# Where the result transposes and the FFN2 tiles live in PSUM: a block-sparse attention and FFN kernel on one core

## The chip, the cores and the metric

One Trainium2 chip, one NeuronCore. The metric is the device time of one execution in microseconds. The kernel before took 329.12 us (median of three runs, 328.71 to 329.84). TensorE, VectorE, ScalarE, GpSimd and the queue engine are written PE, DVE, ACT, POOL and SP, as in the profile.

## The reference

```python
scores = scale * np.matmul(q, k.transpose(0, 1, 3, 2))   # B 4, H 8, S 768, D 64
mask = (|blk_i - blk_j| <= 1) | first/last block row or column | 3 sampled blocks per block row
attn = softmax(np.where(mask, scores, -1e9));  attn_out = attn @ v
x = attn_out.transpose(0, 2, 1, 3).reshape(3072, 512)
h = x @ w_in;  g = 0.5 * h * (1.0 + erf(h * inv_sqrt2));  out = g @ w_out   # d_ff 2048
```

Blocks are 32 positions; a block row sees 8 blocks of keys (first, last, three around it, three sampled), only the first and last block rows see all 24.

## The kernel before

Every engine executes its own queue in the order in which the program is written (`manual_schedule`); the tile pools only add the semaphore waits. So the order in which the Python functions call each other is the order on each engine, and an engine that waits holds up all that is behind it in its queue.

**Units.** The work is cut into nine units of query rows: units 0, 1 and 2 are the three parts of batch 0 (128, 256 and 384 rows), then two units of 384 rows per batch. Units 0, 3, 5 and 7 are "dense": they also compute the first and last block row. A quad is 128 rows, four blocks.

**Stages.** The main loop runs over n = 0 to 8. Stage n computes FFN1 of unit n (`ffn1_step`, eight steps of eight products and one gelu on ACT), then `attention` of unit n+1, into which the FFN2 products of unit n are strewn as filler: `ffn2_pieces` yields once per product (16 products of 128x512 make one quad's output tile `op`), and `fill(m)` takes m of them. The lists in QUOTAS and in the last lines of the loop say how many pieces go behind each iteration (quota, the first entry for iteration -1) and how many into the tail behind the last one. After attention the pieces left are run, then FFN1 of unit n+1 begins; its first product needs all of the transposed attention result xT.

**One attention.** A round is two block rows of one quad, or for dense units one block row and half the heads; I write S, E, T for a round's scores (PE, L287), exponentials (ACT, L324, four per round) and transposes of the probabilities (DVE, L341/345), V for the product of probabilities and values of a group (PE, L387 or L363), F for filler pieces (PE, L447). Rounds count from 0. A group is the two rounds of one quad (g0, g1, g2), or the four dense rounds (d). Iteration `it` of `attention` issues, each on its engine: S of round it+1; V of a group that is two rounds old; T of round it-1; the maxima (DVE, L312/315) of round it+1; the division (DVE, L400 to 404, tile xh) of the group just weighed; E of round it; hooks; filler; and `outputs` of the group that was weighed the iteration before. `outputs` transposes xh on PE (L414) into the PSUM tile `tx`, and ACT copies it to xT (L419, L424). Behind the loop stand the load of the gelu table on ACT, the last T, the V of the last group, and the last `outputs`.

**PSUM.** Eight banks: psA (two tiles of two banks: scores and FFN1 results), psV (one tile of two banks, `av`: the values), psT (one bank: `tx`), psO (one bank: `op`). A pool with one buffer makes the next writer wait for the last reader of the tile before.

**The store.** When the last piece of a quad's tile is issued, `store` at once issues the copy `os<-op` on ACT (L439) and the DMA on SP (L441).

**Gathers.** Sampled blocks are copied by number into the tile gb (`gather`, L251), three copies per block row, mostly on DVE; the block numbers come from registers (`block_numbers`). For unit 2, six block rows are gathered during FFN1 of unit 1 and five in hooks of its attention (QUOTAS n = 1). GpSimd gathers four block rows for unit 1 at the start. GpSimd also issues all loads, each of which can wait for an older one.

**In front of stage 0.** Unit 0's attention runs alone with no filler; its hook at iteration 5 puts a large copy on ACT (`kvs[0][:, :, 0:KC]` from k0, L545).

**The end.** `last_output` computes FFN2 of unit 8 without anything beside it: two full quads and one in two halves, in four banks.

Of the kernel before, what the change touches and what calls it, by code (L numbers as in the profile page):

```python
# [9 lines left out]
F32 = mybir.dt.float32  # L10
# [9 lines left out]
def kernel(  # L20
# [22 lines left out]
    V2 = 2 * VW  # L43
    KC = NPR * BL
# [19 lines left out]
    psT = ctx.enter_context(tc.tile_pool(name="psT", bufs=1, space=PSUM))  # L64
    psO = ctx.enter_context(tc.tile_pool(name="psO", bufs=1, space=PSUM))
# [50 lines left out]
    def load_w_out(part, n=2):  # L116
        w = KOUT // n
        nc.gpsimd.dma_start(
            out=w_out_sb[:, w * part:w * part + w, :],
            in_=moe_w_out[P * w * part:P * w * (part + 1)].rearrange("(ko p) f -> p ko f", p=P))  # L120
# [92 lines left out]
    def spaces():  # L213

        views = [psT.tile([P, PI, PP], BF16, name="pt", tag="T")]
        two = psV.tile([P, 2, 1024], BF16, name="pq", tag="V")
        views += [two[:, i, 0:S].rearrange("p (i c) -> p i c", i=PI) for i in range(2)]
        return views + [psO.tile([P, PI, PP], BF16, name="pt", tag="op")]
# [176 lines left out]
    def divided(grp):  # L395
# [11 lines left out]
        st[grp, "xh"] = xh, n, m  # L407

    def outputs(unit, grp):
        xh, n, m = st.pop((grp, "xh"))  # L410
        T = psT.tile([P, 4, P], BF16, name="tx", tag="T")
        for h in range(2):
            for G in range(m // 2):
                nc.tensor.transpose(T[:, 2 * G + h, 0:32 * n],  # L414
                                    xh[0:32 * n, h, P * G:P * G + P],
                                    identity[0:32 * n, 0:32 * n])
        if grp[0][0] == "s":
            xT, t0 = column[unit.b, grp[0][1][0]]
            nc.scalar.copy(xT[:, :, t0:t0 + 32 * n], T[:, :, 0:32 * n])  # L419
        else:  # L420
            Tv = T[:, 0:2, :].rearrange("p h (g x q) -> p g h x q", g=2, x=2)
# [5 lines left out]
    def ffn1_step(n, m):  # L427
# [6 lines left out]
        nc.scalar.activation(g[:, m:m + 2, 0:T], hp[:, :, 0:T], AF.Gelu)  # L434
# [7 lines left out]

    def ffn2_pieces(n):
        for t, quad in enumerate(units[n].quads):
            op = psO.tile([P, D_MODEL], F32, name="op")
            for m in range(KOUT):
                nc.tensor.matmul(op, lhsT=g[:, m, t * P:(t + 1) * P], rhs=w_out_sb[:, m, :],  # L447
                                 start=(m == 0), stop=(m == KOUT - 1))
                if m != KOUT - 1:
                    yield  # L450
            store(n, quad, slice(0, D_MODEL), op)
            yield

    def last_output(n):
# [5 lines left out]
        banks = [psO.tile([P, D_MODEL], F32, name="op"), two[:, 0, :], two[:, 1, :],  # L460
                 psT.tile([P, D_MODEL], F32, name="op", tag="T")]
# [7 lines left out]
    def attention(unit, filler, quota, tail, held=0, hooks=None):  # L469
# [14 lines left out]
        for it in range(-1, n):  # L484
# [11 lines left out]
            if it >= 0:  # L496
                exponentials(rounds[it])
            for f in hooks.get(it, ()):
                f()
# [4 lines left out]
        while due and due[0][0] < n - 1:  # L504
            divided(weigh())
            if len(given) > 1:
                outputs(unit, given.pop(0))
        turned(rounds[n - 1])
        fill(tail[0])
        divided(weigh())  # L510
        while len(given) > 1:
            outputs(unit, given.pop(0))
        fill(tail[1])
        outputs(unit, given.pop(0))
        for _ in filler:
            pass

# [15 lines left out]
    for part in range(2):  # L533
        load_w_out(part)
# [12 lines left out]
    QUOTAS = {0: ([0, 2, 4, 4, 1], (1, 2)), 1: ([6, 5, 5, 4, 3, 2, 2], (1, 2))}  # L547
    for n, unit in enumerate(units):
# [3 lines left out]
        hooks = {}  # L552
        if nxt is not None and not fresh:
# [4 lines left out]
            elif n == 1:  # L558
                known |= block_numbers(J1[:6], DVE)
                gather(nxt, J1[:6], known)  # L560
                for it, (i0, i1) in enumerate(((6, 9), (9, 11))):
                    hooks[it] = [lambda u=nxt, js=J1[i0:i1]: gather(u, js, block_numbers(js, DVE))]
# [4 lines left out]
        for s in range(KOUT // 2):  # L567
            ffn1_step(n, 2 * s)
            if s == 0:
                if n == 0:  # L570
                    hold_loads(0)
                    for h in range(H):
                        load_v(1, h)
                if n > 0 and not fresh and b + 1 < B:
# [29 lines left out]
        elif n in QUOTAS:  # L604
            attention(nxt, filler, *QUOTAS[n], hooks=hooks)
        elif fresh:
            attention(nxt, filler, [5, 5, 6, 4, 4, 4, 4, 2, 2, 2, 0], (2, 5))
        else:
            attention(nxt, filler, [8, 8, 5, 5, 6, 2, 2], (3, 6))
# [30 lines left out]
```

## Time and profile before

| | us |
|---|---|
| profiled execution, device time | 329.59 |
| its span in the profile | 327.8 |
| median of the timed runs | 329.12 |
| PE busy | 269.1 (82%) |
| DVE busy | 220.1 (67%) |
| ACT busy | 218.9 (67%) |
| POOL busy | 52.6 (16%) |
| granted TensorE clock, mean | 0.984 |

The span is what the trace covers; 1.8 us of the device time lie around it. The stretches of the span, cut near the first product of each FFN1 and the end of the last one (us, PE busy in brackets): unit 0 with the start 33.6 (17.1); FFN1 of unit 0 5.6; attention of unit 1 15.7 (9.5); FFN1 of unit 1 7.6; attention of unit 2 20.6 (14.3); then three times FFN1 14.8 to 15.0, dense attention 28.5, 28.5 and 26.7 (22.4, 23.0, 21.4), FFN1 10.5 to 11.1, sparse attention 19.2, 19.0 and 19.7 (16.8, 16.9, 17.1); and the last output, 14.8. In the FFN1 stretches PE is busy all the time; in the attentions it is not.

In the views below a line of the timeline has start, length, engine, source line, operation, operands, count, and in brackets how long the engine had been idle and what released it. A line of the waits has who waited for whom, the total in us, how often, and the longest.

### The profile page before, as it was taken

What the parts mean: (1) busy time and instruction counts of PE and PEld (TensorE: products, weight loads), DVE (VectorE), ACT (ScalarE), POOL (GpSimd) and SP (SyncE); (2) the same over time, 40 slices, a digit from 0 to 9 for tenths busy, and PEclk for the clock granted to TensorE, in tenths of its full rate; (3) what the DMA queues carried; (4) which work ended last, traced back from release to release, by engine and by line L of the source; (5) the groups of instructions that cost most, each with busy time, mean ns of one, the idle gap of its engine ahead of it and who ended that gap; (6) DMA issues with size and microseconds to landing.
All of it is one profiled execution on the core that took longest, in us unless ns stands there. A gap on an engine that the chain in (4) does not pass through costs nothing.

```text
span 327.8 us, 12763 instructions
## 1 busy us (share of the span) xinstructions
PE 269.1 (82%) x5582; PEld 155.8 (48%) x5624; DVE 220.1 (67%) x553; ACT 218.9 (67%) x378; POOL 52.6 (16%) x100
## 2 busy tenths in 40 slices
PE   1756776967999769988999779988999679979994
PEld 0515624634553445545653445545653445445643
DVE  6497764786597778586597778485698778584000
ACT  9668673767478674686477775686577775777521
POOL 8565900300520002300510002100000000000000
PEclk9999979999999988999999998999999999999999
DMA  7999994930790000930890001911000000000001
GB/s 113 139 123 207 208 113 41 153 76 4 69 64 32 36 4 34 149 80 36 71 62 32 34 6 37 187 39 37 34 3 32 36 4 34 1 36 36 32 34 64
DMA packets 39337, 20.74 MB, mean 63 GB/s; under 512 B 25841, under 2 KB 36338, under 8 KB 39282
## 3 DMA queue, kind: packets, MB, share of 16 engines
q0 software_dynamic: 35680, 13.63, 62.8%
q1 hardware_dynamic: 3602, 6.29, 5.0%
q8 instruction: 44, 0.72, 1.0%
q14 instruction: 11, 0.09, 0.1%
HBM read 27.26 MB, written 6.29 MB: 102 GB/s over the span
## 4 chain that ended last, share of the span: by engine, by line
PE 58%; DVE 15%; ACT 13%; issue 6%; DMA 5%; POOL 1%; DVEq 1%; ACTq 0%; POOLq 0%
PE hp L432 25%; PE op L447 13%; ACT pp L324 8%; PE av L387 6%; DVE pT L341 4%; DVE nm L312 4%; PE sc L287 3%; DMA w_in_sb<-in_moe_w_in_dram 3%; DVE xh L404 3%; DMA kv<-in_v_dram 2%; DVE kv L204 2%; PE av L465 2%; PE pt L193 2%; PE op L465 2%; ACT L351 2%
## 5 line engine op out<-in xcount | busy, mean ns | idle before, releaser
L324 ACT ACTIVATE pp<-sc,nm 128x256 bf16<-128x256 f32 (+1 forms) x192 | 91.8, 592 | 13.6 <-DVE nm L312 11.3
L432 PE MATMUL hp<-xT,w_in_sb 128*128 128x384 bf16 (+2 forms) x576 | 89.3, 312 | 1.2 <-ACT xT L419 0.9
L447 PE MATMUL op<-w_out_sb,g 128*128 128x512 bf16 x295 | 80.3, 390 | 9.4 <-issue 4.8
L434 ACT ACTIVATE g<-hp 128x768 bf16<-128x768 f32 (+2 forms) x72 | 53.2, 739 | 39.6 <-PE hp L432 39.4
L432 PEld LDWEIGHTS <-w_in_sb 128*128 128x128 bf16 x576 | 53.4, 100 | 32.1 <-issue 3.2
L312 DVE TENSOR_REDUCE nm<-sc 128x4 f32<-128x1024 f32 (+1 forms) x48 | 53.3, 1113 | 11.3 <-PE sc L287 10.7
L251 DVE COPY gb<-kv 128x388 bf16 (+1 forms) x252 | 46.0, 262 | 10.2 <-issue 8.6
L447 PEld LDWEIGHTS <-g 128*128 128x128 bf16 x336 | 28.5, 100 | 37.5 <-issue 15.5
L387 PE MATMUL av<-kv,pT 64*32 64x130 bf16 x1760 | 35.0, 229 | 12.8 <-DVE xh L404 5.4
L387 PEld LDWEIGHTS <-pT 64*32 64x32 bf16 x2816 | 29.0, 93 | 23.7 <-DVE xh L404 9.6
L341 DVE STREAM_TRANSPOSE pT<-pp 128x512 f32<-128x512 f32 (+1 forms) x48 | 31.6, 658 | 11.4 <-ACT pp L324 11.0
L287 PE MATMUL sc<-gb,qT 64*32 64x256 bf16 x704 | 19.7, 283 | 15.2 <-ACT pp L324 14.9
L287 PEld LDWEIGHTS <-qT 64*32 64x32 bf16 x832 | 10.8, 90 | 42.9 <-issue 29.1
L419 ACT COPY xT<-tx 128x512 bf16<-128x512 bf16 (+1 forms) x24 | 13.2, 552 | 23.6 <-PE tx L414 23.6
L439 ACT COPY os<-op 128x512 f32<-128x512 f32 (+1 forms) x23 | 13.3, 576 | 19.7 <-PE op L447 15.4
L124 POOL COPY mark<-g 1x1 bf16<-1x1 bf16 x6 | 3.6, 594 | 137.1 <-ACT g L434 137.0
L107 POOL DMA_DIRECT2D kv<-in_v_dram x32 | 22.8, 720 | 5.4 <-DMA w_out_sb<-in_moe_w_out_dram 3.5
L387 PE MATMUL av<-gb,pT 64*32 64x130 bf16 x1056 | 21.3, 230 | 1.4 <-issue 1.3
L351 ACT ACT_TABLE_LOAD x17 | 21.8, 1283 | 0.3
L404 DVE TENSOR_TENSOR xh<-av,rec 128x512 bf16<-128x512 f32 (+2 forms) x28 | 18.3, 652 | 1.0
L400 DVE TENSOR_SCALAR den<-av 128x8 f32<-128x8 f32 (+2 forms) x28 | 4.4, 155 | 21.2 <-PE av L387 20.7
L315 DVE TENSOR_REDUCE nm<-sc 128x1 f32<-128x768 f32 x16 | 15.3, 955 | 4.2 <-PE sc L287 4.0
(63 smaller groups left out, 212.8 us busy)
## 6 DMA issues: line engine op xcount, KB each, us to landing
out_dram<-os SPq DMA_DIRECT2D x23, 256.0 KB, 2.0
kn<-in_k_dram POOLq DMA_DIRECT2D x8, 384.0 KB, 5.5
qn<-in_q_dram POOLq DMA_DIRECT2D x8, 384.0 KB, 8.0
kv<-in_v_dram POOLq DMA_DIRECT2D x32, 96.0 KB, 7.7
w_in_sb<-in_moe_w_in_dram POOLq DMA_DIRECT2D x4, 512.0 KB, 12.7
w_out_sb<-in_moe_w_out_dram POOLq DMA_DIRECT2D x2, 1024.0 KB, 20.4
out_dram<-os SPq DMA_DIRECT2D x2, 128.0 KB, 1.7
raw<-in_sampled_blocks_dram SPq DMA_DIRECT2D x1, 0.6 KB
```

Of the source, the lines that this page charges most:

```text
L107: nc.gpsimd.dma_start(out=kvs[b % 2][32 * hh:32 * hh + 32, 0:NB, c0:c0 + D], in_=v[b, h].rearrange("(n p) d -> p n d", p=BL))
L251: (engine or nc.vector).tensor_copy(sampled(unit.place[j], r)[:, None, c0:c1], src[:, bass.ds(at[j][r], 1), :])
L287: nc.tensor.matmul(o, lhsT=qT[rows, pr, BL * j:BL * j + BL], rhs=rhs(rows, pr), start=True, stop=True)
L312: nc.vector.tensor_reduce(out=nm[:, 0:2 * n].rearrange("p (g j) -> p g j", g=2), in_=A4[:, :, 0:n, :], op=ALU.max, axis=AX.X, negate=True)
L324: nc.scalar.activation(dst.rearrange("p (c k e) -> p c e k", e=2, k=BL), src.rearrange("p (c e k) -> p c e k", e=2, k=BL), AF.Exp, bias=bias)
L341: nc.vector.transpose(pt[:, 0:w].bitcast(F32), pp[:, 0:w].bitcast(F32))
L351: nc.scalar.activation(junk, zero[0:1, 0:1], func)
L387: nc.tensor.matmul(av[32 * s:32 * s + 32, h, V2 * G:V2 * G + V2], lhsT=pv[rows, c // 2, :, c % 2], rhs=src[rows], start=(c == 0), stop=(c ...
L404: nc.vector.tensor_tensor(xh[rows, :, 0:m * D].rearrange("p h (x d) -> p h x d", d=D), a[:, :, :, 0:D], rec[rows, :, 0:m, None].to_broadca ...
L432: nc.tensor.matmul(hp[:, i, 0:T], lhsT=w_in_sb[:, ki, (m + i) * P:(m + i + 1) * P], rhs=xTs[n % 2][:, ki, 0:T], start=(ki == 0), stop=(ki ...
L434: nc.scalar.activation(g[:, m:m + 2, 0:T], hp[:, :, 0:T], AF.Gelu)
L447: nc.tensor.matmul(op, lhsT=g[:, m, t * P:(t + 1) * P], rhs=w_out_sb[:, m, :], start=(m == 0), stop=(m == KOUT - 1))
```

## The change

1. psT is gone. The transposed results go into free columns of the value tile itself: `av` has two banks of 512 columns, the values use 260 of each, and the transposes use 128 columns from column 264 on.
2. psO has two buffers. A finished tile is put on a list and copied out later: behind the exponentials of the next iteration, or at the latest when another tile has been finished.
3. The gelu of the last FFN1 step is two instructions, one for each half.
4. For unit 2, four block rows are gathered on GpSimd behind the value loads of stage 0, and one more on DVE before the attention; the hooks of its attention are gone.
5. w_out is loaded in four parts instead of two.
6. In the tail all given groups are put out before the next one is weighed, and all quotas and tails are new.

```diff
+    TX = 4 * VW + 4
-    psT = ctx.enter_context(tc.tile_pool(name="psT", bufs=1, space=PSUM))
-    psO = ctx.enter_context(tc.tile_pool(name="psO", bufs=1, space=PSUM))
+    psO = ctx.enter_context(tc.tile_pool(name="psO", bufs=2, space=PSUM))
...
-    def load_w_out(part, n=2):
+    def load_w_out(part, n=4):
...
-        views = [psT.tile([P, PI, PP], BF16, name="pt", tag="T")]
+        views = [psO.tile([P, PI, PP], BF16, name="pt", tag="op")]
...
-        T = psT.tile([P, 4, P], BF16, name="tx", tag="T")
+        T = av[:, :, TX:TX + P].bitcast(BF16).rearrange("p h (g t) -> p g h t", g=2)
         for h in range(2):
             for G in range(m // 2):
-                nc.tensor.transpose(T[:, 2 * G + h, 0:32 * n],
+                nc.tensor.transpose(T[:, G, h, 0:32 * n],
...
-        nc.scalar.activation(g[:, m:m + 2, 0:T], hp[:, :, 0:T], AF.Gelu)
+        for i in ((0, 2),) if m < KOUT - 2 else ((0, 1), (1, 2)):
+            nc.scalar.activation(g[:, m + i[0]:m + i[1], 0:T], hp[:, i[0]:i[1], 0:T], AF.Gelu)
...
+    finished = []
+
     def ffn2_pieces(n):
         for t, quad in enumerate(units[n].quads):
+            store_finished(1)
             op = psO.tile([P, D_MODEL], F32, name="op")
...
-                if m != KOUT - 1:
-                    yield
-            store(n, quad, slice(0, D_MODEL), op)
-            yield
+                if m == KOUT - 1:
+                    finished.append((n, quad, slice(0, D_MODEL), op))
+                yield
+
+    def store_finished(left=0):
+        while len(finished) > left:
+            store(*finished.pop(0))
...
-        banks = [psO.tile([P, D_MODEL], F32, name="op"), two[:, 0, :], two[:, 1, :],
-                 psT.tile([P, D_MODEL], F32, name="op", tag="T")]
+        banks = [psO.tile([P, D_MODEL], F32, name="op") for _ in range(2)] + [two[:, 0, :], two[:, 1, :]]
...
             if it >= 0:
                 exponentials(rounds[it])
+            store_finished()
...
         table(AF.Gelu)
-        while due and due[0][0] < n - 1:
-            divided(weigh())
-            if len(given) > 1:
-                outputs(unit, given.pop(0))
         turned(rounds[n - 1])
         fill(tail[0])
-        divided(weigh())
-        while len(given) > 1:
-            outputs(unit, given.pop(0))
+        while due:
+            while given:
+                outputs(unit, given.pop(0))
+            divided(weigh())
         fill(tail[1])
         outputs(unit, given.pop(0))
         for _ in filler:
             pass
+        store_finished()
...
-    for part in range(2):
+    for part in range(4):
         load_w_out(part)
...
-    QUOTAS = {0: ([0, 2, 4, 4, 1], (1, 2)), 1: ([6, 5, 5, 4, 3, 2, 2], (1, 2))}
+    QUOTAS = {0: ([4, 4, 2, 2, 1], (1, 1)), 1: ([6, 5, 5, 4, 3, 1, 1], (3, 2))}
...
-                for it, (i0, i1) in enumerate(((6, 9), (9, 11))):
-                    hooks[it] = [lambda u=nxt, js=J1[i0:i1]: gather(u, js, block_numbers(js, DVE))]
+                gather(nxt, J1[6:7], block_numbers(J1[6:7], DVE))
...
+                    gather(units[2], J1[7:], block_numbers(J1[7:], POOL), engine=nc.gpsimd)
...
-            attention(nxt, filler, [5, 5, 6, 4, 4, 4, 4, 2, 2, 2, 0], (2, 5))
+            attention(nxt, filler, [4, 4, 4, 4, 4, 4, 3, 3, 2, 2, 1], (6, 4))
-            attention(nxt, filler, [8, 8, 5, 5, 6, 2, 2], (3, 6))
+            attention(nxt, filler, [8, 8, 5, 5, 5, 2, 2], (6, 4))
```

## The prediction

> **What bounds the kernel now.** I read the busy line and the windows by stage first, then the waits, then the timeline of one stage of each kind.
>
> ```profile
> PE 269.1 (82%) x5582; PEld 155.8 (48%) x5624; DVE 220.1 (67%) x553; ACT 218.9 (67%) x378; POOL 52.6 (16%) x100
> ```
>
> PE is the busiest engine, and in the FFN1 stretches it never rests. What can be won or lost lies in the attentions, where PE idles 5 to 6 us in a dense one, 2 to 3 in a sparse one of batches 1 to 3, and 6 in unit 2's.
>
> ```profile
> ACT xT L419 <- PE tx L414: 23.6, 17, 3.1
> PE sc L287 <- ACT pp L324: 16.7, 20, 2.6
> ACT os L439 <- PE op L447: 15.4, 16, 2.2
> PEld L387 <- DVE xh L404: 9.6, 9, 1.8
> PE op L447 <- ACT os L439: 4.0, 12, 0.4
> ```
>
> The third and fifth lines are what the second bank aims at: ACT stands at a copy of op until the tile is done (15.4 us), PE waits 4.0 us for those copies. The fourth is the present price of one value bank: V of the next group waits until xh has been read out of it.
>
> The start of stage 0, then a sparse attention, then a dense one, from the timeline:
>
> ```profile
> 26.93 2.86 ACT L545 COPY kv<-qT 128x3200 bf16<-128x3200 bf16 x1
> 28.91 0.62 PE L387 MATMUL av<-kv,pT 64*32 64x130 bf16 x28 [0.32 <-DVE pT L341]
> 29.81 1.28 ACT L351 ACT_TABLE_LOAD   x1
> 31.10 0.20 ACT L351 ACTIVATE junk<-zero 1x1 bf16<-1x1 bf16 x1
> 31.46 0.43 ACT L424 COPY xT<-tx 128x128 bf16<-128x128 bf16 x2 [0.16 <-PE tx L414]
> 33.61 5.17 PE L432 MATMUL hp<-xT,w_in_sb 128*128 128x128 bf16 x64 [0.68 <-ACT xT L419]
> ```
>
> ```profile
> 148.96 0.59 PE L447 MATMUL op<-w_out_sb,g 128*128 128x512 bf16 x2 [0.44 <-ACT os L439]
> 149.39 0.38 PE L414 MATMUL tx<-identity,xh 128*128 128x128 bf16 x4
> 149.71 0.42 PE L387 MATMUL av<-kv,pT 64*32 64x130 bf16 x32
> 150.36 0.60 ACT L419 COPY xT<-tx 128x512 bf16<-128x512 bf16 x1
> ```
>
> ```profile
> 258.40 0.58 ACT L439 COPY os<-op 128x512 f32<-128x512 f32 x1 [2.16 <-PE op L447]
> 258.88 1.72 ACT L324 ACTIVATE pp<-sc,nm 128x256 bf16<-128x256 f32 x4
> 263.53 0.34 PE L414 MATMUL tx<-identity,xh 96*128 96x96 bf16 x4
> 264.09 0.49 ACT L419 COPY xT<-tx 128x384 bf16<-128x384 bf16 x1
> ```
>
> In the first and second of these, V of the next group (L387) starts before ACT has copied the transposes of the group before it. With T in the same tile as av it can't: the order of instructions after the change puts an ACT wait on the first V product of every group behind another. That is the step I follow.
>
> **Unit 0: +2.9 us.** ACT's queue stays: the copy L545 (26.93 to 29.79), the gelu table and its junk activation (to 31.30), then the two xT copies of group d (0.43). V of g0 now waits for them: 31.3 + 0.43 + 0.06 (ACT to PE, as 33.56 to 33.61) = 31.8 against 28.91. V takes 2.1 us as before, and xh, transposes, copy and FFN1 follow in a chain without slack. So 2.9 later, nothing hides it: there is no filler, and the next stages start from here.
>
> **Sparse attentions of units 4, 6, 8: +1.1 us each.** I follow unit 4. What goes: the waits for os at both tile changes (0.33 and 0.44), and 0.38 at S3, since E1 no longer stands behind os. What comes first: ACT now runs E0, E1, os, E2. E0 starts at 139.5 (0.1 late, below), lasts 1.67; E1 to 142.85; os 0.59; E2 1.66, to 145.1, so S4 starts at 145.15 against 145.37. F5, S5 and F2 follow: transposes of g0 at 148.75 against 149.39, 0.24 of which is one piece less in the quota. Then the copy: it starts 0.44 after the first transpose (154.35 to 154.79), lasts 0.58, and 0.06 later V of g1 starts, at 149.8 against 149.71. Left: +0.1 and one piece owed (0.24). In the tail the transposes of g1 now stand between V of g1 and V of g2, and PE waits the same 0.7 (1.08 less 0.38 of transposing) once more: V of g1 to 151.05; eight pieces to 153.1; V of g2 at 154.2, and with 1.05 for 96 products to 155.25; four pieces, 1.0, are less than the 1.3 that den, rec and xh take (154.35 to 155.63), so the last transposes start at 156.6; three pieces cover the copy, FFN1 at 157.65. Before it was 156.78 with 0.45 of "issue" idle inside V of g2; +0.9 without and +1.3 with such a stall: 1.1.
>
> **Dense attentions of units 3, 5, 7: +0.7 us each.** Unit 7 (granted clock 1.00). E2 starts at 250.05, not 250.75, and E6 at 257.1, not 258.88 (the os copies are no longer ahead of them); S8 moves from 260.65 to 259.45, V of g0 to 260.05 (waiting 0.2 for its copies), S9 from 262.55 to 261.75. Up to here 0.8 is won, though with fewer pieces done. Now V of g1: the copy of g0's transposes stands on ACT behind E8 and the second os (order after the change): E8 from 261.8 to 263.5, os to 264.05, copy to 264.55, V of g1 at 264.6, while PE was done at 263.2. V of g1 ends at 265.85, before 265.68, and 34 pieces are done, not 38. Tail as above: seven pieces to 267.65, transposes, copy (table loaded by 267.85) to 268.7, V of g2 to 270.0, xh to 271.3, transposes, copy, FFN1 at 272.4 against 271.74.
>
> **Unit 1: +0.3.** S3 comes 0.6 earlier (two pieces ahead of it, not four), E3 ends at 47.6, but V of g1 must wait for table (1.48) and copy (0.48): 49.75 against 49.47.
>
> **Unit 2: -1.2.** The nine hook copies (66.50, 1.76 with 1.04 of register loads before them) held T0 and so the maxima of round 2 from about 66.65 to 68.81; the six others cost about 0.9 again. Twelve copies go to POOL, three (0.6, and some 0.4 of register load) ahead of the attention, where the table load (62.73 to 64.01) hides them. With E2 at 67.95, E3 at 70.2, E4 at 71.9, V of g1 starts at 74.25 against 75.88. Then the tail's copy wait and xh chain: FFN1 at 81.3 against 83.15, or 82.3 without the 0.86 "issue" idle there; between -1.9 and -0.5, I take -1.2.
>
> **Small edits.** The gelu: 128x512 takes 597 ns, 128x256 384, so 171 are fixed; two halves cost 171 more, less an overlap of up to 155 (exponentials of 546 follow each other every 0.39). Only the first half has a wait on PE in the order after the change, so it waits for the whole step: 0 to +0.1, hidden mostly behind fillers, and counted above; -0.3 a stage if I misread the wait. w_out in quarters: before, it landed at 38.2 and 44.2; two more issues (0.88 each) delay POOL's gathers to about 28.4, before the 29.85 at which they wait for ACT anyway: nothing. POOL copies: 283 ns at 128 columns and 415 at 260 give about 0.54 at 388; twelve are 6.5 us at about 46 to 53, needed at 70: nothing. End: the fourth bank now waits for a copy of half a tile (0.37) where the third waited for a whole one (0.59): -0.2.
>
> **Sum.** 2.9 + 3 x 1.1 + 3 x 0.7 + 0.3 - 1.2 - 0.2 = 7.2. Against the profiled execution's 329.59 that is 336.8; the median lies 0.47 below that execution, so I predict 336 us.
>
> **Rivals.**
> *Half of it (330 to 332).* Unit 0's wait stands, but the tails cost nothing, because the "issue" stalls (1.19 at 118.5, 0.45 at 153.2) fall into the new waits. For: the tails hold such stalls. Then 2.9 + 0.3 - 1.2 - 0.2, about +2: 331.5. Chance 0.15.
> *Faster, 326.* ACT's relief is the larger part. If ACT reaches the copies so early that V never waits, which decides from 1.4 us ahead of my schedule in a dense stage and 0.7 in a sparse one, the leads worked out above remain: 0.8 at S9, 0.64 at the first transposes, and 2.3 in unit 2: 2.9 + 0.3 - 0.2 - 2.4 - 1.9 - 2.3 = -3.6. For: 15.4 us of ACT idle time. Against: the copies stand behind exponentials and table in ACT's queue. Chance 0.17; 0.06 more that the two balance.
> *POOL and DVE get in each other's way.* A DVE copy begun beside a POOL copy at 33.87 took 0.94 us where a like one right after took 0.78, so up to 0.2 a copy; the twelve would have to slip by 4 us to meet the fixed gathers of unit 2. Worth up to 12 x 0.2 = 2.4, 339. Chance 0.02.
> The Trainium skill (SBUF — State Buffer, Who interferes with whom) has a harder rule: a VectorE copy in a two-port mode and a GpSimd instruction lock each other out for a whole instruction. By it twelve collisions would cost 12 x 0.54 = 6.5 us, and the sum would be 343; the trace shows no full lockout, since five DVE copies of 128x384 beside POOL's copies (32.2 to 33.8) average 340 ns and two without them 336.
>
> **Chances and range.** The forecast, 332.5 to 340: 0.60. A measurement of this kernel tells about 0.3% from no change. Slower 0.60 + 0.15 + 0.02 = 0.77, same 0.06, faster 0.17. The range from 328.5 to 340 leaves out most of the faster case and little above.
>
> **What would show it.** The first FFN1 product near 36.5 instead of 33.61, with V of unit 0's second group released by ACT xT. A new line "av L387 <- ACT xT" in the waits, near 10 us; the lines "os <- op" and "op <- os" almost gone. Dense attentions longer by 0.7, sparse by 1, unit 2's shorter by 1. I am wrong if V behind another group starts without waiting for the copy, or if ACT idles before those copies instead of being late.

## The result, and the profile after

The changed kernel takes **324.61 us** (median of four runs, 324.14 to 325.28) beside 328.91 us of the kernel before on the same chip (four runs, 327.28 to 329.84). The ratio is 0.9876, 95% interval 0.9832 to 0.992. I had predicted 336.0 us, slower. It is faster, and below my range.

The profiled execution took 325.28 us, its span is 323.5, and its mean granted clock is 1.00 (before 329.59, 327.8 and 0.984). The waits of the page after, engine and line, then whom it waited for, total in us, times and longest:

```profile
ACT xT L419 <- PE av L414: 31.4, 15, 3.9
PE av L387 <- ACT xT L419: 12.9, 15, 1.3
PE sc L287 <- ACT pp L324: 11.7, 17, 1.2
PE av L387 <- ACT xT L425: 3.5, 4, 3.0
ACT os L441 <- PE op L452: 1.3, 4, 0.8
```

The second and fourth lines are the new wait that the prediction followed: V stands until ACT has copied the transposes out of the value bank. Together they are 16.4 us, where I expected some 10. The wait of PE for os is gone, that of ACT for op fell from 15.4 to 1.3. So the forecast wait is there, and more of it than forecast, and the kernel is still faster. Where the time went is seen by stage. I cut both traces at the first FFN1 product and the first score product of each stage (us; the FFN1 stretches not listed, 14.81 and 10.49, are equal to 0.01 before and after). The last two columns are experiments that come below. A second profile of the change, `after_again` below, differs by 0.42 or less in every stage but one: FFN1 of unit 1 took 9.04 there, with the granted clock at one half from 54.5 to 61.3. So the change doesn't always have the 7.11 of the table.

| | before | after | difference | forecast | banks of before, new counts and gathers | banks by kind |
|---|---|---|---|---|---|---|
| start to FFN1 of unit 0 | 33.61 | 37.08 | +3.47 | +2.9 | 33.38 | 33.59 |
| FFN1 of unit 0 | 5.19 | 6.05 | +0.86 | 0 | 5.71 | 6.05 |
| attention of unit 1 | 16.10 | 14.31 | -1.79 | +0.3 | 15.94 | 16.35 |
| FFN1 of unit 1 | 7.11 | 7.11 | 0 | 0 | 7.11 | 8.40 |
| attention of unit 2 | 21.14 | 19.03 | -2.11 | -1.2 | 18.94 | 18.53 |
| dense, unit 3 | 28.64 | 27.15 | -1.49 | +0.7 | 27.80 | 29.20 |
| sparse, unit 4 | 19.69 | 19.52 | -0.17 | +1.1 | 19.92 | 19.52 |
| dense, unit 5 | 28.43 | 26.61 | -1.82 | +0.7 | 24.83 | 25.37 |
| sparse, unit 6 | 19.52 | 19.47 | -0.05 | +1.1 | 20.07 | 19.48 |
| dense, unit 7 | 26.88 | 26.12 | -0.76 | +0.7 | 25.03 | 24.78 |
| sparse, unit 8 | 20.18 | 19.99 | -0.19 | +1.1 | 20.25 | 19.74 |
| from FFN1 of unit 8 to the end | 25.41 | 25.12 | -0.29 | -0.2 | 25.40 | 25.10 |
| span | 327.8 | 323.5 | -4.3 | +7.2 | 320.3 | 322.1 |

Three stretches of the timeline after, the counterparts of those shown of before: unit 0, the sparse attention of unit 4, the dense one of unit 7 (start, length, engine, line, operation, count, and in brackets the idle time and what ended it).

```profile
27.88 2.86 ACT L551 COPY kv<-qT 128x3200 bf16<-128x3200 bf16 x1 [1.07 <-DVE gb L251]
30.75 1.28 ACT L351 ACT_TABLE_LOAD   x1
32.16 0.40 ACT L425 COPY xT<-av 128x128 bf16<-128x128 bf16 x2
32.60 0.64 PE L387 MATMUL av<-kv,pT 64*32 64x130 bf16 x32 [2.97 <-ACT xT L425]
```

```profile
147.63 0.59 ACT L419 COPY xT<-av 128x512 bf16<-128x512 bf16 x1
148.27 0.42 PE L387 MATMUL av<-kv,pT 64*32 64x130 bf16 x32 [0.67 <-ACT xT L419]
149.47 1.90 PE L452 MATMUL op<-w_out_sb,g 128*128 128x512 bf16 x8
151.21 0.39 PE L414 MATMUL av<-identity,xh 128*128 128x128 bf16 x4
152.26 0.41 PE L387 MATMUL av<-kv,pT 64*32 64x130 bf16 x24 [0.67 <-ACT xT L419]
```

```profile
258.77 0.34 PE L414 MATMUL av<-identity,xh 96*128 96x96 bf16 x4
260.37 0.42 PE L387 MATMUL av<-kv,pT 64*32 64x130 bf16 x32 [1.25 <-ACT xT L419]
261.56 1.68 PE L452 MATMUL op<-w_out_sb,g 128*128 128x512 bf16 x7
264.30 0.42 PE L387 MATMUL av<-kv,pT 64*32 64x130 bf16 x32 [0.83 <-ACT xT L419]
```

In each of them V starts just behind the end of the copy (148.22 to 148.27 in the second), never ahead of it, as it could before. The waits are near the forecast ones: 0.67 a group in a sparse attention, where I had 0.7, and 1.25 for V of g1 in the dense one, where I had 1.4 (PE done at 263.2, V at 264.6). What is missing from my sums is gain.

### The profile page after: what moved, and what is told of

The parts are those of the page before. It is cut to its first block, busy times and chain, and to the rows that moved or that the text cites. A ratio compares the mean times of both kernels' runs of the same rounds, so it can differ in the third digit from the quotient of the medians.

```text
span 323.5 us, 12843 instructions
## 1 busy us (share of the span) xinstructions
PE 268.1 (83%) x5624; PEld 153.7 (48%) x5624; DVE 217.2 (67%) x541; ACT 219.7 (68%) x387; POOL 60.5 (19%) x114
## 4 chain that ended last, share of the span: by engine, by line
PE 49%; ACT 23%; DVE 15%; issue 5%; DMA 5%; POOL 1%; DVEq 0%; ACTq 0%; POOLq 0%
PE hp L433 26%; ACT pp L324 11%; PE av L387 7%; PE op L452 6%; ACT L351 4%; DVE nm L312 4%; DMA w_in_sb<-in_moe_w_in_dram 3%; DVE xh L404 3%; ACT xT L419 3%; DMA kv<-in_v_dram 2%; PE op L472 2%; ACT g L436 2%; PE av L414 2%; DVE nm L315 2%; DVE kv L204 2%
## 5 line engine op out<-in xcount | busy, mean ns | idle before, releaser
L452 PE MATMUL op<-w_out_sb,g 128*128 128x512 bf16 x336 | 86.8, 381 | 1.2 <-issue 1.2
L436 ACT ACTIVATE g<-hp 128x768 bf16<-128x768 f32 (+4 forms) x81 | 53.8, 676 | 40.5 <-PE hp L433 40.5
L433 PEld LDWEIGHTS <-w_in_sb 128*128 128x128 bf16 x576 | 54.5, 102 | 32.6 <-issue 4.0
L387 PE MATMUL av<-kv,pT 64*32 64x130 bf16 x1760 | 29.9, 225 | 17.0 <-ACT xT L419 12.9
L452 PEld LDWEIGHTS <-g 128*128 128x128 bf16 x336 | 26.7, 97 | 34.0 <-issue 10.1
L419 ACT COPY xT<-av 128x512 bf16<-128x512 bf16 (+1 forms) x24 | 13.2, 551 | 31.6 <-PE av L414 31.4
L124 POOL COPY mark<-g 1x1 bf16<-1x1 bf16 x6 | 4.9, 812 | 128.6 <-ACT g L436 128.6
L387 PE MATMUL av<-gb,pT 64*32 64x130 bf16 x1056 | 20.0, 226 | 0.6 <-issue 0.6
L441 ACT COPY os<-op 128x512 f32<-128x512 f32 x23 | 13.4, 584 | 6.9 <-PE op L472 5.5
L414 PE MATMUL av<-identity,xh 128*128 128x128 bf16 (+1 forms) x104 | 10.4, 221 | 8.9 <-DVE xh L404 8.8
```

What stands on the lines that cost most here:

```text
L387: nc.tensor.matmul(av[32 * s:32 * s + 32, h, V2 * G:V2 * G + V2], lhsT=pv[rows, c // 2, :, c % 2], rhs=src[rows], start=(c == 0), stop=(c ...
L419: nc.scalar.copy(xT[:, :, t0:t0 + 32 * n].rearrange("p (g h) t -> p g h t", g=2), T[:, :, :, 0:32 * n])
L433: nc.tensor.matmul(hp[:, i, 0:T], lhsT=w_in_sb[:, ki, (m + i) * P:(m + i + 1) * P], rhs=xTs[n % 2][:, ki, 0:T], start=(ki == 0), stop=(ki ...
L436: nc.scalar.activation(g[:, m + i[0]:m + i[1], 0:T], hp[:, i[0]:i[1], 0:T], AF.Gelu)
```

## The theories, and the experiments

**Theory A:** the shared bank costs about what its waits show, 7 us or more, and other parts of the change (filler counts, the gathers on GpSimd, the second bank with its later copy) win more than that. **Its rival:** the shared bank costs little, because its waits take the place of stalls that were there before, and the gain comes of ACT's relief alone. Each kernel was timed against the kernel before on its own chip; "first, second, third, fourth" are four such groups, in which the kernel before took 329.73, 329.85, 329.01 and 329.05 us. Numbers from one group are compared directly, others by their ratios.

### The shared bank alone (first group)

```diff
--- before
-        T = psT.tile([P, 4, P], BF16, name="tx", tag="T")
+        T = av[:, :, TX:TX + P].bitcast(BF16).rearrange("p h (g t) -> p g h t", g=2)
...
-        divided(weigh())
-        while len(given) > 1:
-            outputs(unit, given.pop(0))
+        while due:
+            while given:
+                outputs(unit, given.pop(0))
+            divided(weigh())
```

> The kernel before with one part of the change: the transposed results in free columns of the value tile, and the order of the tail that this needs; one FFN2 bank, copies at once, the quotas of before. Theory A (the waits of V for the xT copies are the price that the forecast gave, and the second FFN2 bank with its later copies brings more than it): slower than before by 2.9 us in unit 0 and 0.5 to 1 in each of the eight other attentions, 7 to 11 us in all. Theory B (the waits cost little, because PE gets them back elsewhere, and the new quotas or the clock bring the gain): slower by unit 0's 3 us alone.

Measured: 338.51 us (337.08 to 339.01), ratio 1.0254 (1.0203 to 1.0304), **+8.8 us**. The sparse attentions take 20.81, 20.87 and 21.51, 1.1 to 1.35 more than before, unit 0 is 2.3 later. So the new wait is dear, and the rival is out as an account of the whole: what I had priced is real, as long as nothing else of the change is there. Two other things are mixed into the 8.8. Five stretches of 3.4 us inside this run went at half clock, three before. And PE's gaps of over 0.4 us that the profile calls "issue" sum to 1.2 us (1.2 in the change, 4.7 before), so some stalls did give way to waits, as the rival says, but far too few to pay for them.

### The filler counts, and the gathers on GpSimd, without the banks (third and fourth group)

```diff
--- before: filler counts alone
-    QUOTAS = {0: ([0, 2, 4, 4, 1], (1, 2)), 1: ([6, 5, 5, 4, 3, 2, 2], (1, 2))}
+    QUOTAS = {0: ([4, 4, 2, 2, 1], (1, 1)), 1: ([6, 5, 5, 4, 3, 1, 1], (3, 2))}
...
-            attention(nxt, filler, [5, 5, 6, 4, 4, 4, 4, 2, 2, 2, 0], (2, 5))
+            attention(nxt, filler, [4, 4, 4, 4, 4, 4, 3, 3, 2, 2, 1], (6, 4))
...
-            attention(nxt, filler, [8, 8, 5, 5, 6, 2, 2], (3, 6))
+            attention(nxt, filler, [8, 8, 5, 5, 5, 2, 2], (6, 4))
--- before: gathers alone
-                    hooks[it] = [lambda u=nxt, js=J1[i0:i1]: gather(u, js, block_numbers(js, DVE))]
+                gather(nxt, J1[6:7], block_numbers(J1[6:7], DVE))
...
+                    gather(units[2], J1[7:], block_numbers(J1[7:], POOL), engine=nc.gpsimd)
```

> The kernel before with the quotas and tails of after and nothing else. Theory C (the pieces moved behind the loop keep PE's clock from being halved in the tails of the dense units, which the two kernels with the old tails and one bank showed in five of six dense tails): 1 to 3 us faster than before, the dense attentions near 27 us without half clock, the sparse ones no better than before. Theory A (only the banks and copies matter): within 1 us of before.

> The kernel before with the gathers of unit 2 on GpSimd (and one block row ahead of the attention) and nothing else. Forecast's step: unit 2's attention about 2 us shorter (19 instead of 21.1), 1 to 2.5 us faster in all. Rival (with one FFN2 bank the attention of unit 2 is held by other waits): within 0.5 us.

> The kernel before with the changed filler counts and with the GpSimd gathers of unit 2, and with nothing of the banks: transposes in their own bank, one FFN2 bank copied at once, the tail order of before. Alone the two gave -2.6 and -1.5. If they add up, it is 4.1 below before, about 325, and the whole bank swap is worth less than 1 us net: what it wins in the sparse attentions it pays in unit 0 and in the dense ones. If instead the swap is a real gain of the change (its second bank and later copies won 5.4 within the change), this kernel must stay 2 or more above the change, at 327 or over. Attentions: unit 2's near 18.7, dense 24.8, sparse 19.9 to 20.5, first FFN1 at 33.6 to 33.9.

Measured: filler counts alone 326.41 us (324.05 to 327.91), ratio 0.9942 (0.9905 to 0.9979), **-2.6**. Gathers alone 327.48 (325.09 to 329.12), ratio 0.9944 (0.9908 to 0.9979), **-1.5**, with the attention of unit 2 at 18.66 us instead of 21.14. Both, in the fourth group: 323.78 (322.07 to 324.93), ratio 0.9827 (0.978 to 0.9874), **-5.3**. That is no slower than the whole change: the kernel with the banks of before and these two edits has the lower ratio, and the intervals overlap. The moved banks as a whole won nothing that can be measured.

The dense attention of unit 7 shows what the counts do. PE's timeline of the kernel before, then of the one with the new counts alone, from V of g1 to V of g2:

```profile
263.80 0.75 PE L387 MATMUL av<-kv,pT 64*32 64x130 bf16 x32
...
265.84 0.38 PE L447 MATMUL op<-w_out_sb,g 128*128 128x512 bf16 x1 [0.16 <-issue]
266.92 0.24 PE L387 MATMUL av<-kv,pT 64*32 64x130 bf16 x4 [0.70 <-DVE xh L404]
```

```profile
259.94 0.75 PE L387 MATMUL av<-kv,pT 64*32 64x130 bf16 x32
...
261.45 1.69 PE L447 MATMUL op<-w_out_sb,g 128*128 128x512 bf16 x7
263.06 0.24 PE L387 MATMUL av<-kv,pT 64*32 64x130 bf16 x4
```

Both take 3.12 us from V to V. Before, PE runs two pieces (one has no record) and waits 0.70 for xh in there; with the new counts seven pieces lie in that time for nothing. They no longer stand further ahead: 34 pieces are done by V of g1, not 38, and it starts 17.23 us after the first score product of the stage, not 18.95. Four pieces at 0.22 us each are 0.9 of these 1.7, and they are not all of it. The same counts decide how long ACT stands at its copies of finished tiles, here again before and with the new counts alone:

```profile
250.27 0.58 ACT L439 COPY os<-op 128x512 f32<-128x512 f32 x1 [1.04 <-PE op L447]
258.40 0.58 ACT L439 COPY os<-op 128x512 f32<-128x512 f32 x1 [2.16 <-PE op L447]
```

```profile
249.09 0.58 ACT L439 COPY os<-op 128x512 f32<-128x512 f32 x1 [0.26 <-PE op L447]
258.50 0.59 ACT L439 COPY os<-op 128x512 f32<-128x512 f32 x1
```

With the old counts ACT reaches the copies 1.04 and 2.16 us before the tile's last piece is done, and the next exponentials stand behind them; with the new ones 0.26 and nothing. Over the whole run that wait falls from 15.4 to 2.6 us by the counts alone, with one bank and copies at once; the line of the waits there is

```profile
ACT os L439 <- PE op L447: 2.6, 9, 0.5
```

So the counts bring most of the relief of ACT that the second bank and the later copy were made for.

The attention is 24.78 us instead of 26.88, at the full clock in both. The changed kernel has the same counts and takes 26.12, so beside the new counts the bank costs 1.3. Beside the old ones it does not: the change with the old counts, below, takes 26.76 in unit 7. There the later copy relieves ACT and pays for the bank, and the new counts add only 0.64 to it. The two remedies overlap, and what each is worth depends on whether the other is there.

### The second bank, the later copy, and the counts and gathers taken back (first and second group)

```diff
--- after: one FFN2 bank, copied at once
-    psO = ctx.enter_context(tc.tile_pool(name="psO", bufs=2, space=PSUM))
+    psT = ctx.enter_context(tc.tile_pool(name="psT", bufs=1, space=PSUM))
+    psO = ctx.enter_context(tc.tile_pool(name="psO", bufs=1, space=PSUM))
--- after: two banks, copied at once (also in the kernel above)
-            store_finished(1)
...
-                if m == KOUT - 1:
-                    finished.append((n, quad, slice(0, D_MODEL), op))
-                yield
+                if m != KOUT - 1:
+                    yield
+            store(n, quad, slice(0, D_MODEL), op)
+            yield
```

> The kernel after, but with a single FFN2 bank, whose tile is copied at once when its last piece is issued, as before; the freed bank is used only where the kernel before used its own transpose bank outside attention. All else as after. Theory A (the second bank and the later copy carry the gain): 7 to 10 us slower than after, so slower than before, with the PE waits for os (0.33 and 0.44 a tile) and ACT's waits at os back (about 15 us). Theory B (quotas or clock carry it): within 1.5 us of after.

> The kernel after with its two FFN2 banks, but the copy of a finished tile is issued at once, ahead of the next exponentials, as before. It tells the bank from the delay. Theory A1 (it is ACT standing at os that held back the exponentials): 3 to 5 us slower than after, ACT's wait for op back at over 10 us, PE's wait for os still gone. Theory A2 (it is PE's wait for the bank): within 1 us of after. Theory B: within 1 us of after too, and the one-bank kernel also.

The next three are the change once more, the change with the old counts (the diff of the counts above, backwards), and the change with unit 2's gathers back on DVE (that of the gathers, backwards).

> The kernel after, unchanged, beside the three others of this group on one chip. 324 to 325.5 us, granted clock 0.995 or more in most executions, if the four runs shown with it were typical; if its clock was luck, some executions will show 0.97 to 0.99 and 326 to 328 us.

> The kernel after with the quotas and tails of before; the tail's order, both banks, the later copies and GpSimd's gathers stay. Theory C (the pieces placed in the tails fill PE while the copies and divisions run, and keep its clock from being halved there): 3 to 6 us slower than after, with longer PE waits for xT and xh in the tails and one or two stretches of half clock in the tails of the dense units. Theory A (the banks and the later copies carry the gain alone): within 1.5 us of after, clock as after.

> The kernel after with unit 2's last five block rows gathered on DVE in the hooks of its attention, as before. Forecast's step for unit 2: 1.5 to 2.5 us slower than after, the attention of unit 2 back to 20 us or more. Rival (DVE's copies were hidden, the gain of unit 2 came from an instruction stall of PE that went): within 0.7 us.

Measured: one bank 330.48 us (328.89 to 333.15), ratio 1.0024 (0.9989 to 1.0058). Two banks with the copy at once 327.43 (326.37 to 330.37), ratio 0.9956 (0.9922 to 0.9989). In the sparse attentions of units 4, 6 and 8 that is 21.09, 21.04, 21.86 with one bank, 20.31, 20.27, 20.74 with two, 19.52, 19.47, 19.99 with the later copy: 0.8 a stage each. The dense one of unit 7 is 26.11, 26.12 and 26.12: nothing, once the counts are new. The steps are smaller in the total than the expectations had them (7 to 10 and 3 to 5 above the change): they are 4 to 5, and about 2. The change again 325.58 (324.72 to 327.1), ratio 0.9896 (0.9836 to 0.9956). With the old counts 327.52 (325.25 to 329.92), ratio 0.9961 (0.9914 to 1.0008), about 2 more on the same chip, though the intervals overlap; the expectation had 3 to 6. With the gathers on DVE 329.75 (326.92 to 331.39), ratio 0.9999 (0.9955 to 1.0042), 4.2 more; the attention of unit 2 is 22.64 instead of 18.91, with hook copies like these, from its timeline:

```profile
70.45 1.76 DVE L251 COPY gb<-kv 128x388 bf16 x9 [1.05 <-issue]
73.87 1.09 DVE L251 COPY gb<-kv 128x388 bf16 x6
```

Not all of the 3.7 in that stage is theirs: the clock was at one half there from 81.0 to 84.4, and in the kernel before the same gathers were worth 2.5 in this stage and 1.5 in all.

So the steps from before to after are, taken in this order and by ratio and chip: shared bank +8.8; counts, gathers and the small edits -8.0 on top of it; second bank -3.1; later copy about -2. Another order would give other terms, as unit 7 shows. The bank pays for itself in the sparse attentions by what the bank set free there, and in the dense ones, beside the new counts, it only costs.

### Unit 0: its wait, the loads of w_out, and the clock (first to fourth group)

```diff
--- after: unit 0's transposes in a bank of their own
+        if unit is units[0]:
+            T = psO.tile([P, 2, 2, P], BF16, name="tx", tag="op")
--- after: w_out in halves (alone, and beside the first edit with the gelu whole)
-    def load_w_out(part, n=4):
+    def load_w_out(part, n=2):
--- both, and unread products in the attentions of units 0 and 1
+                nc.tensor.matmul(spare, lhsT=kn[0:PP, 0, 0:P], rhs=kn[0:PP, 0, 0:D_MODEL],
+                                 start=True, stop=True)
```

> The kernel after, but unit 0, which has no FFN2 filler, puts its transposes in an FFN2 bank instead of the value tile. Theory A: V of its second group no longer waits for ACT's copies, so FFN1 of unit 0 starts near 34.5 instead of 37.1, 2.5 to 3.5 us are won, and it is faster than both kernels, 321 to 322 us. Rival (the later stages absorb the wait of unit 0, since loads end at fixed times): 0 to 1 us won.

> The kernel after with three parts undone at the start: unit 0's transposes in an FFN2 bank, w_out in two parts, the last gelu whole. If w_out in quarters made GpSimd's twelve copies meet DVE's twelve in unit 0 (2.94 us for them instead of 1.98), FFN1 of unit 0 starts near 33 us, 4 us earlier than in after. Theory D (PE's clock is halved for as long again when unit 1 leaves PE idle, so time won in unit 0 is given back before FFN1 of unit 1 ends): 324.5 to 326 us in all, with half clock between 45 and 60 us. Rival (what is won in unit 0 stays): 320.5 to 321.5 us.

> The kernel after with w_out loaded in two parts as before. If the two issues more pushed GpSimd's copies into DVE's twelve copies of unit 0 (1.98 us before, 2.94 after): those 1.98 again, FFN1 of unit 0 at 36.1 instead of 37.05, 0 to 1 us faster than after. Rival (they met by chance): no difference in the start of FFN1.

> The change with w_out in two loads once more, for a comparison on the same chip: 323.0 to 324.5, 1 to 1.5 below the change; the twelve DVE copies of unit 0 take 1.9 to 2.0 us and the first FFN1 product is at 36.1. If the gain of the first run was chance, 324.6 to 326.

> The kernel of unit0_w_out_gelu with 30 products more that nobody reads, on data that lies there, in idle gaps of PE in the attentions of units 0 and 1 (12 and 17); the output is the reference's. Theory D (PE's clock is halved for lack of work in the window before): full clock earlier than 36 us and no half clock between 45 and 65 us, FFN1 of unit 0 nearer to 4 us than to 5.3, FFN1 of unit 1 back to 7.1 from 9.4; 2.5 to 5 us faster than unit0_w_out_gelu, 319 to 322 us. Rival (the halving is set by something else, as the loads that run then): no gain, or a loss of up to 1 us for the products in the way.

Measured, unit 0 with its own bank: 325.57 us (323.63 to 326.5), ratio 0.9863 (0.9813 to 0.9913). The first FFN1 product comes at 33.87, 3.2 earlier, so the shared bank does make unit 0 late; but the time is that of the change, not the 321 to 322 of the expectation. In this kernel the profile shows the clock at one half from 51.9 to 58.8, and the attention and FFN1 of unit 1 take 15.86 and 8.56 us, not 14.31 and 7.11. With the two edits beside it: 324.4 (322.89 to 325.45), ratio 0.9862 (0.98 to 0.9925), half clock from 49.7 to 59.9.

The halves of w_out alone gave 323.72 (322.73 to 327.97), ratio 0.9829 (0.9775 to 0.9882), and in the fourth group 325.86 (324.15 to 329.05), ratio 0.9876 (0.9826 to 0.9926), that of the change itself: no gain that two groups agree on. But unit 0 shows a cost that I had put at nothing. The twelve fixed gathers on GpSimd and on DVE, in the timeline of the change and of the halves again (one of GpSimd's twelve there falls ahead of the view; the kernel before stands between them, GpSimd from 22.70 to 25.58 and DVE 1.98 us from 24.91):

```profile
24.88 2.88 POOL L251 COPY gb<-qT 128x128 bf16 x12 [0.51 <-issue]
24.91 2.94 DVE L251 COPY gb<-kv 128x260 bf16 x12
```

```profile
21.87 2.66 POOL L251 COPY gb<-qT 128x128 bf16 x11
24.90 1.72 DVE L251 COPY gb<-kv 128x260 bf16 x12
```

The four loads make GpSimd late, its copies fall on DVE's, and these take 1.2 us longer than alone, 0.96 longer than before, ahead of ACT's large copy and all that follows; the first FFN1 product comes at 37.08 instead of 35.86. The Trainium skill (SBUF — State Buffer, Who interferes with whom) says that a DVE copy in a two-port mode and GpSimd shut each other out for whole instructions, which by an estimate from the durations here would cost DVE up to 2.88 us; the trace agrees that they meet, and shows 1.2.

The unread products (29 are in the kernel, not the 30 of the expectation): 326.19 us (324.42 to 327.03), ratio 0.9897 (0.9843 to 0.995), far from the 319 to 322 that theory D gave. What D says of the clock held at first: FFN1 of unit 0 is 4.46 us instead of 5.3 to 6.0, and FFN1 of unit 1 7.11 instead of 9.41, both at the full clock. But the attention of unit 1 takes 18.98, with half clock from 52.9 to 56.3, a wait for w_out and this stall of PE, from its timeline:

```profile
52.61 0.24 PE L387 MATMUL av<-gb,pT 64*32 64x130 bf16 x5 [2.23 <-issue]
```

and later stretches fall to half clock instead (from 76.8 and 189.4, 3.4 us each). These three kernels start FFN1 3.2 to 3.9 us earlier than the change, and by the end of unit 2's attention they stand at 83.2, 83.0 and 84.5 us. The change stands at 83.6 in its first profile and at 85.2 in its second, so most of what was won is lost again by then; the times of the three can't be told from that of the change.

### Banks dealt by kind of attention (fourth group)

```diff
--- after, with w_out in halves and the gelu whole
+        if unit.dense:
+            T = psT.tile([P, 2, 2, P], BF16, name="tx", tag="T")
...
+            two_banks = not own and t % 2
+            op = (psT.tile([P, D_MODEL], F32, name="op", tag="T") if two_banks
+                  else psO.tile([P, D_MODEL], F32, name="op"))
...
+                    if own:
+                        store(n, quad, slice(0, D_MODEL), op)
+                    else:
+                        finished.append((n, quad, slice(0, D_MODEL), op))
```

> The change with the banks dealt by kind of attention: in a dense one (and in units 0 and 1's own order) the transposes have their own bank, one FFN2 bank, copied at once, and the tail order of before; in a sparse one the transposes share the value bank, two FFN2 banks, copied a step later. w_out in two loads, gelu whole. If the terms by stage add up: unit 0 at 33.7 (-3.4 against the change), dense near 24.8 (-1.3 each, -3.9), sparse 19.5 (0), unit 2's 18.7 (0), less 2 to 4 for stretches at half clock around unit 1, which came in each kernel that won time in unit 0: 318 to 321. If what is won in one stage is always lost in a later one (clock, or waits that fall into each other), it is 323 to 326, no better than the change with w_out in halves.

Measured: **322.69 us** (321.99 to 323.86), ratio 0.9788 (0.974 to 0.9835), the lowest of all. The last column of the table gives its profiled run, the longest of the five: sparse 19.5 to 19.7 and dense 24.8 to 25.4 in units 5 and 7 as expected, but unit 3 at 29.20 (half clock for 6.8 us, and a stall of 2.3 at 118.9) and unit 1 with 16.35 and 8.40 (half clock for 6.8 us). So the terms hold in the stages that ran at the full clock; what unit 0 won, 3.5, unit 1 gives back but for 0.2, and unit 3 loses some 4. The time lies between my two expectations and meets neither: 318 to 321 had allowed 2 to 4 for the clock already. Against the 323.78 of the banks of before it is 1.1 less, in intervals that overlap.

## The clock, seen in the windows

In each trace the recorded clock changes only at whole multiples of 3.41 us from the first entry on, so a trace can be cut on that grid. Columns: stretch, its length, busy time of PE, PE's weight loads, DVE, ACT and POOL (count), granted clock, DMA share and GB/s. First three stretches of the kernel before, each the 3.4 us ahead of one in which the clock was halved (42.7, 121.2 and 196.3), and a fourth in unit 7's tail, after which it was not. Then two of the kernel with the banks by kind, ahead of its halvings at 51.9 and 120.2, and one of unit 7.

```profile
39.30:42.70 3.40, 0.95 (x26) 0.35 (x28) 2.20 (x3) 3.39 (x8) 1.64 (x3) 1.00 1.54 193
117.80:121.20 3.40, 1.36 (x89) 0.82 (x73) 2.32 (x6) 2.78 (x5) 0.00 (x0) 1.00 0.03 5
192.90:196.30 3.40, 1.86 (x132) 1.36 (x132) 1.47 (x4) 2.34 (x5) 0.00 (x0) 1.00 0.02 5
264.56:267.98 3.42, 1.82 (x124) 1.19 (x125) 2.95 (x6) 2.69 (x6) 0.00 (x0) 1.00 0.02 5
```

```profile
48.50:51.90 3.40, 1.18 (x80) 0.99 (x81) 0.68 (x2) 1.73 (x3) 3.40 (x9) 1.00 1.24 24
116.80:120.20 3.40, 1.32 (x6) 0.51 (x6) 1.83 (x5) 2.85 (x6) 0.00 (x0) 0.99 0.00 0
260.11:263.52 3.41, 2.61 (x128) 1.54 (x116) 2.73 (x6) 3.00 (x6) 0.00 (x0) 1.00 0.02 5
```

PE was busy 1.0 to 1.9 of the 3.4 us ahead of each halving shown, and 1.8 and 2.6 in the two that no halving followed. All 17 profiles together give 1,385 such stretches at the full clock. PE was busy for less than 1.5 us in 34 of them, and the clock was halved behind all 34; between 1.5 and 1.9 us it was halved behind 8 of 25; above 1.9, behind none of 1,326. So in this case the busy time of PE within the grid's stretch nearly decides, with a band from 1.5 to 1.9 in which the profile doesn't tell (a few products have no record). The two stretches of 1.86 and 1.82 above lie in the band: the first lost the clock, the second kept it. The halved stretches last 3.4, 6.8 or 10.2 us, and one costs a dense attention 1.5 to 2 us: 28.43 for unit 5 before, 26.88 for unit 7. That links the filler counts to the clock in the dense tails: pieces there keep PE busy where it waits for xh. Over all profiled runs, 8 of the 12 dense attentions with the old counts had a halving in their tails, and 2 of the 39 with the new ones. In the total it is not seen: with the new counts alone the mean granted clock of the timed runs is 0.976 (median), before 0.978 in that group; in its profile two stretches were halved, both in unit 1's attention (45.1 and 55.3).

The clock also tells why FFN1 of unit 0 differs from kernel to kernel. Its products in the second profile of the change, up to the first stretch at the full clock and behind it:

```profile
37.04:40.84 3.80, 3.80 (x37) 3.80 (x37) 0.50 1.23 204
40.84:42.78 1.94, 1.92 (x30) 1.62 (x28) 1.00 1.87 171
```

The columns are those of PE and its weight loads. Most products start 107 ns apart in the first line, 56 in the second. The same two spacings stand in the first profile of the change and in the one before, and change at the first entry of their records, 41.74 and 35.87; ahead of that entry the granted clock is not recorded.

The Trainium skill (TensorE: Matmul & The Clock Gate, HAM oscillation — how this bites in real kernels) gives the rule of no idle gap of PE above about 3.4 us; the traces here differ, since in unit 3's tail before no gap of PE was above 1.2 us. No run here varied the busy share by itself, so the band stands as it was seen in these kernels.

## Why the prediction was wrong

**Unit 0, "+2.9": right in kind, +3.47.** V waited 2.97 us for ACT as described, but the bank by itself made FFN1 2.3 late (35.91 with the shared bank alone), so 2.9 was somewhat high. Most of the rest is the step "w_out in quarters: nothing", which was wrong by 0.96: GpSimd's copies met DVE's, the mechanism of the third rival, in unit 0 and not in unit 2 where I had looked for it; for unit 0 I had asked only whether GpSimd would be done in time. FFN1 of unit 0 at +0.86 had no term; its 64 products take 6.12 us here and 5.17 before, both above the 4.29 of the kernel with unread products. They ran 107 ns apart until the full clock came, for 4.7 us here and 2.3 before.

**"Sparse attentions +1.1 each": the step that failed first, -0.05 to -0.19.** The waits stood: two waits of 0.67 for the copy, and one of 0.30 for the last xh. The size is off by 1.2. The runs give its terms: the bank alone costs 1.1 to 1.35 a stage, the new counts alone 0.2 to 0.6, and the second bank and the later copy win 0.8 each. On my schedule, 0.5 us is lead: the first transposes of unit 4 come 11.18 us after its first scores, not 11.66 (before, 12.30). Another 0.3 is the price of pieces: eight in the tail at 2.05 us, where 151.21 less 149.47 is 1.74. I had read "0.16 <-issue" ahead of the filler groups of before as idle time of PE. It is a product without a record: the costliest groups of the page before list the same line twice, and the products are fewer than their weight loads,

```profile
L447 PE MATMUL op<-w_out_sb,g 128*128 128x512 bf16 x295 | 80.3, 390 | 9.4 <-issue 4.8
L447 PEld LDWEIGHTS <-g 128*128 128x128 bf16 x336 | 28.5, 100 | 37.5 <-issue 15.5
```

where the page after has 336 of both. So a group shown as four pieces in 1.03 us held five, and 0.256 a piece, eight times, was my 2.05. The first line of the prediction's own fence said it already, 5582 products for 5624 loads. The rest is 0.2 in the last hand-overs, and 0.2 that I had added for a stall (1.1, between 0.9 and 1.3).

**"Dense attentions +0.7 each": the step that cost most, -0.76 to -1.82.** I followed the bank's waits and charged the counts only as pieces moved from here to there, "34 pieces done, not 38". But the pieces moved into the tail lie in a wait that was there anyway, and the new counts also end ACT's waits of 1.04 and 2.16 us for op. My schedule gave that relief to the later copy and had S9 of unit 7 come 0.8 earlier within its stage. It comes 0.97 earlier with the later copy and the old counts, so that term was sized well; 1.69 with the new counts alone; and 1.62 in the change. Of the 1.46 by which the forecast misses unit 7, this lead is 0.8, and the price of the seven tail pieces, 1.80 where they took 1.52, is 0.3. In terms of runs: the counts by themselves are worth -2.1 in unit 7, the bank beside them costs 1.3, and the sum is what unit 7 shows. Units 3 and 5 add the clock that their tails no longer lose. The granted clock was in the table of before at 0.984, and I gave it no term.

**"Unit 2 -1.2": right in sign, -2.11**, just beyond my bound of -1.9. The same gathers in the kernel before give -2.48 in this stage. In all they win 1.5 in the kernel before, and cost 4.2 when they are taken out of the change, where a stretch at half clock adds to it. **"Unit 1 +0.3": -1.79.** V of g1 comes 10.74 us after the first scores, 10.67 before, so the step itself was right to 0.2. The gain lies behind it, a stall in PE's issue before, which is not there after:

```profile
52.01 0.30 PE L387 MATMUL av<-kv,pT 64*32 64x130 bf16 x14 [1.68 <-issue]
```

That fits the mechanism of the rival "Half of it" for this stage. Over whole runs too, such gaps above 0.4 us sum to 4.7 to 6.3 us in the four kernels with the banks of before, and to 0.8 to 3.2 in the eleven with the shared bank and without unread products. What causes such stalls stays open: the profile names nothing that PE waited for, they move from run to run, and they are as large as 2.2 us in unit 3 with the banks of before and the new counts. **The end, "-0.2": -0.29**, right. **The halved gelu** was never run by itself, so what it does isn't known.

So the forecast's new wait came as described, and the steps that failed are the gains beside it: the counts, charged as a small cost where they win 2.1 a dense attention, and the second bank and later copy in the sparse ones. The rival "Faster, 326" came within 1.4 us of the time, but by luck: its condition, that V never waits, did not hold, since V waited 16.4 us. I worked out the cost of what the change is named after, line by line, and took its side edits at face value; two of these carry by themselves as much as the whole result.

## What to carry to other kernels

When a change moves filler along with its main edit, price the filler by the wait that it falls into: seven pieces lay in the 3.12 us that two had taken before. And ask which copy waits for the last piece of a tile, and what stands behind that copy. A shared bank serialises writer and reader at every hand-over, so give it only to the stages in which the freed bank ends a wait of its own that nothing cheaper ends; beside the new counts those were the sparse attentions, not the dense ones. And run the side edits without the main one early: the single kernel with two of them showed that the moved banks won nothing that could be measured.

## What the runs showed of the hardware

Three things were new to me. The clock was halved for one to three stretches of 3.4 us behind every stretch with PE busy under 1.5 us, behind none above 1.9, and behind some in between, without a pause of PE over 1.2 us in one case; in the kernel with the shared bank alone five such stretches, 17 us, went at half rate. Twelve DVE copies beside GpSimd copies took 2.94 us, alone 1.72. And a product that is missing from a trace shows as 0.16 us of "issue" idle, which is told apart by counting products against weight loads.
